# A gated recurrence feeding a SiLU MLP on one core: the planner that orders the instructions is replaced, and the DMA transposes begin at the eleventh unit

## The chip, the cores and the metric

The kernel runs on one NeuronCore of a Trainium2 chip. The metric is device microseconds of one execution, the median of several runs; lower is better. The core has four compute engines that run side by side, each strictly in the order in which its instructions stand: TensorE (PE, matrix multiplies), ScalarE (ACT, activations), VectorE (DVE) and GpSimd (POOL). SyncE (SP) computes nothing here; it issues DMAs. POOL issues DMAs too.

## The reference

Inputs `q`, `k`, `v`, `f_logit` are float32 of shape (4 batches, 8 heads, 768 steps, 48). The first part is a recurrence with a decay for each key row; its output becomes the input of an MLP with `w_in` (384 x 2048) and `w_out` (2048 x 384):

```python
f = 1.0 / (1.0 + np.exp(-f_logit))
for t in range(S):
    state = f[:, :, t, :, None] * state + np.einsum('bhd,bhe->bhde', k[:, :, t], v[:, :, t])
    y[:, :, t] = np.einsum('bhd,bhde->bhe', q[:, :, t], state)
x = y.transpose(0, 2, 1, 3).reshape(B * S, H * D)      # 3072 x 384
h = x @ w_in
out = (h * (1.0 / (1.0 + np.exp(-h)))) @ w_out          # 3072 x 384
```

## The kernel before, in words

**Units.** The 768 steps are cut into 6 chunks of 128, for each of the 4 batches: 24 units, numbered chunk by chunk, so that unit u needs the state that unit u-4 left. Two neighbouring units make a pair; there are 12 pairs. A unit is 128 rows of the MLP's input.

**What a unit does** (short names as in the planner, lines of the kernel before):
- four loads `f k q v` by SP (L390), 192 KB each;
- `E`, `L` on ACT: exp and log of `f_logit`, the log of the decay (L397, L399); for the first two pairs unit by unit, later for both units of a pair at once;
- `cs` on PE: running sums of that log by a triangular matrix, into the PSUM tile `cs`, of which there is one buffer (L445, L449);
- `ia`, `al`, `a` on ACT: the exponentials of those sums (L452, L456, L454); `a` writes back into the tile `cs`;
- `ki` and `vb` on POOL (k scaled, L458; v cast, L460); `qg` on DVE (q scaled, L462). `qg` is the last reader of the tile `cs`, so the next unit's `cs` waits for it;
- the scaled q and k turned by 90 degrees into `qkT`: either `tq` on PE (eight transposes, L468) and a copy `qkc` on DVE (L470), or `qkD`, one transposing DMA issued by SP (L472);
- `sc` on PE (scores, L479), `at` on DVE (mask, L483), `y` on PE (L488 for the part from the state, L492), `yc` on DVE (L496);
- y turned into `xT`: either `yT` on PE (L502) and `xc` on DVE (L504), or `xD`, a transposing DMA of SP (L498);
- `d` on PE (L510), `sd` on DVE (L515), `su` on POOL (L521): the state's update.

**The MLP.** For a pair (256 rows): eight tasks `mi` on PE, six matmuls of 256 columns each (L426), each followed by `si` on ACT, a SiLU of 128x512 (L422). Then for each unit four tasks `mo` on PE, four matmuls of 384 columns each (L436), a copy `oc` on DVE (L439) and a store `so` (L442), issued by POOL up to unit 17 and by SP from unit 18. The PSUM tile `mlp` has three buffers. `mi` tile j needs a quarter of `w_in`, `mo` step m a quarter of `w_out`: eight DMAs `wi`, `wo` of 384 KB issued by POOL (L409, L412).

**Tables.** Exp and log share one table of ACT, SiLU has another. Every change of kind on ACT puts a table load there (L549).

**Who sets the order.** A planner runs when the kernel is built. `make_tasks` (L61) lists all tasks with their engine, an assumed cost and their dependences; `schedule` (L174) plays a greedy list schedule: whenever an engine is free it takes the ready task of least priority number. A priority is a due time: `pace` (3.66 in the kernel before) times the unit's number plus an offset of the kind of task (`rank`). Buffers are given out in the same play. SP and POOL each have a ring of DMAs; where both have one under way, SP's gets 0.17 of the rate. `margin` is added on the way into PE. `planned` (L323) sorts the tasks by their planned start, and the kernel emits them in that order (L545), inside `tc.manual_schedule()`. What is handed to the chip is only the order on each engine, and which buffer each task uses: the chip waits on semaphores, not on planned times.

**Idle matmuls.** 70 matmuls on a tile of zeros (`warm`, L414) are tasks with the worst priority of all; PE takes one when it has nothing else, until they are used up. All stand before the first `mi`.

**Orders around the change, as built.** On SP the loads go `f0 k0 q0 v0 f1 k1 q1 v1 ...` up to `f12`, then turns (`qkD`, `xD`) stand between them. On POOL the weights stand after `vb2` (three of `wi`), after `su0` (`wi3`, `wo0`), after `su1` (`wo1`), after `ki4` (`wo2`) and after `vb6` (`wo3`): `w_after` in the configuration ties each to a `ki`. On ACT the `E` of a pair may stand ahead of an `a` or `L` that other work waits for: `ia17 E20 al17 a17`, `E16 E18 L16 L18 ia16`.

Of the kernel before, what the change touches and what calls it, by code (L numbers as in the profile page):

```python
# [21 lines left out]
NTILES = 16  # L22

CFG = dict(
    turned=8,
    turned_y=8,
    warm=70,
    warm_at=5.0,
    single=0,
    w_after=(2, 2, 2, 3, 3, 3, 4, 5),  # L30
    pace=3.66,
    margin=0.2,
    late_store=18,
    keep_exp=117.43,
    keep_silu=245.53,
    hold_exp=0.58,
    hold_silu=0.64,
    rank=dict(ld=-44.14, E=-215.27, cs=-365.49, ia=97.44, ki=-23.12, vb=175.4, qg=451.56, tq=-142.94, qkc=-77.52, sc=-74.11, at=-79.38, y=-7.63, yc=-223.81, yT=-176.78, xc=-369.47, d=13.22, sd=-254.14, su=26.79, mi=-117.59, si=-4.81, mo=20.95, mstep=0.47, oc=215.45, so=524.34, wi=23.7, wo=55.81),
# [5 lines left out]
ENGINES = ("PE", "ACT", "DVE", "POOL", "SP")  # L44
SEM = {"PE": 0.22, "ACT": 0.06, "DVE": 0.06, "POOL": 0.08, "SP": 0.0}
INTO_PE = 0.09
TABLE = 1.29


class Task:  # L50
    def __init__(self, name, eng, occ, lat, prio, deps=(), acq=(), use=(), mode=None, dma=0.0):
        self.name, self.eng, self.occ, self.lat, self.prio = name, eng, occ, lat, prio
        self.deps, self.acq, self.use, self.mode, self.dma = list(deps), list(acq), list(use), mode, dma
# [6 lines left out]

def make_tasks(cfg):  # L61
    T, tasks, pace, R = {}, [], cfg["pace"], cfg["rank"]
    extra = cfg.get("extra", {})

    def add(name, eng, occ, lat, prio, **kw):
        t = Task(name, eng, occ, lat, prio + extra.get(name, 0.0), **kw)
        T[name] = t
        tasks.append(t)
        return t
# [8 lines left out]
    base = lambda u: pace * u  # L78
    for n in range(cfg["warm"]):
        add(("warm", n), "PE", 0.107, 0.107, 1e6 + n, acq=[inst(("wm", n), "mlp")])  # L80
    for u in range(UNITS):
        P = u // 2
        for n, x in enumerate("fkqv"):
            add((x, u), "SP", 0.45, 0.45, base(u) + R["ld"] + n * 0.1, acq=[inst((x, P), x)], dma=0.875)

    for P in range(PAIRS):
        us_list = [(2 * P,), (2 * P + 1,)] if P < 2 else [(2 * P, 2 * P + 1)]
        for us in us_list:
            occ, lat = (0.43, 0.54) if len(us) == 1 else (0.74, 0.85)
            e = add(("E", us), "ACT", occ, lat, base(us[0]) + R["E"], deps=[T["f", u] for u in us], acq=[inst(("e", us), "e")],  # L90
                    use=[I["f", P]], mode="exp")
            add(("L", us), "ACT", occ, lat, base(us[0]) + R["E"] + 0.1, deps=[e], acq=[inst(("lf", P), "lf")],
                use=[I["e", us]], mode="exp")
    log_of = lambda u: T["L", (u,)] if u < 4 else T["L", (u - u % 2, u - u % 2 + 1)]

    for u in range(UNITS):
        c, b, P, B = u // BATCHES, u % BATCHES, u // 2, base(u)
# [5 lines left out]
        occ = 0.162 + (0 if last else 0.1)  # L103
        cs = add(("cs", u), "PE", occ, occ, B + R["cs"], deps=[log_of(u)], acq=[I["cs", u]], use=[I["lf", P]])
        ia = add(("ia", u), "ACT", 0.387, 0.49, B + R["ia"], deps=[cs], acq=[I["ia", u]], use=[I["cs", u]], mode="exp")
        if not last:
            al = add(("al", u), "ACT", 0.08, 0.173, B + R["ia"] + 0.1, deps=[cs], acq=[I["al", u]], use=[I["cs", u]], mode="exp")
        a = add(("a", u), "ACT", 0.387, 0.486, B + R["ia"] + 0.2, deps=[ia], use=[I["cs", u]], mode="exp")
        ki = add(("ki", u), "POOL", 0.94, 0.994, B + R["ki"], deps=[ia, T["k", u]], acq=[I["qk", u]], use=[I["ia", u], I["k", P]])
        vb = add(("vb", u), "POOL", 0.445, 0.503, B + R["vb"], deps=[T["v", u]], acq=[I["vb", u]], use=[I["v", P]])  # L110
        qg = add(("qg", u), "DVE", 0.47, 0.554, B + R["qg"], deps=[a, T["q", u]], acq=[I["qk", u]], use=[I["cs", u], I["q", P]])
        if u >= cfg["turned"]:
            qkT = add(("qkD", u), "SP", 0.6, 0.6, B + R["tq"], deps=[qg, ki], acq=[I["qkT", u]], use=[I["qk", u]], dma=1.3)
        else:
            tq = add(("tq", u), "PE", 0.444, 0.444, B + R["tq"], deps=[qg, ki], acq=[I["tq", u]], use=[I["qk", u]])
            qkT = add(("qkc", u), "DVE", 0.61, 0.692, B + R["qkc"], deps=[tq], acq=[I["qkT", u]], use=[I["tq", u]])
        sc = add(("sc", u), "PE", 0.425, 0.33, B + R["sc"], deps=[qkT], acq=[I["sc", u]], use=[I["qkT", u]])
        at = add(("at", u), "DVE", 1.2, 1.29, B + R["at"], deps=[sc], acq=[I["atm", u]], use=[I["sc", u]])
        yd = [at, vb] + ([T["su", u - BATCHES]] if c else [])
        y = add(("y", u), "PE", 0.38 if c else 0.21, 0.38 if c else 0.21, B + R["y"], deps=yd, acq=[I["y", u]],  # L120
                use=[I["atm", u], I["vb", u], I["qkT", u]] + ([I["st", u - BATCHES]] if c else []))
        yc = add(("yc", u), "DVE", 0.475, 0.558, B + R["yc"], deps=[y], acq=[I["yb", u]], use=[I["y", u]])
        if u >= cfg["turned_y"]:
            xc = add(("xD", u), "SP", 0.4, 0.4, B + R["yT"], deps=[yc], acq=[I["xT", P]], use=[I["yb", u]], dma=0.6)
        else:
            yT = add(("yT", u), "PE", 0.167, 0.167, B + R["yT"], deps=[yc], acq=[I["yT", u]], use=[I["yb", u]])
            xc = add(("xc", u), "DVE", 0.27, 0.358, B + R["xc"], deps=[yT], acq=[I["xT", P]], use=[I["yT", u]])
        T["x", u] = xc
        if not last:
            d = add(("d", u), "PE", 0.168, 0.168, B + R["d"], deps=[ki, vb, y], acq=[I["d", u]], use=[I["qk", u], I["vb", u]])  # L130
            sdd = [d] + ([T["su", u - BATCHES]] if c else [])
            sd = add(("sd", u), "DVE", 0.464, 0.551, B + R["sd"], deps=sdd, acq=[I["sd", u]],
                     use=[I["d", u]] + ([I["st", u - BATCHES]] if c else []))
            add(("su", u), "POOL", 1.01, 1.07, B + R["su"], deps=[sd, al], acq=[I["st", u]], use=[I["sd", u], I["al", u]])

    for n in range(4):
        add(("wi", n), "POOL", 0.8, 0.8, R["wi"] + n, deps=[T["ki", cfg["w_after"][n]]], dma=2.36)
    for n in range(4):
        add(("wo", n), "POOL", 0.8, 0.8, R["wo"] + n, deps=[T["ki", cfg["w_after"][4 + n]]], dma=2.5)

    for P in range(PAIRS):
        B = base(2 * P + 1)
        single = P < cfg["single"]
        for j in range(NTILES // 2):
            us = [(2 * P + i,) for i in range(2)] if single else [(2 * P, 2 * P + 1)]
            pass
        parts = [(2 * P,), (2 * P + 1,)] if single else [(2 * P, 2 * P + 1)]
        per = 4 if single else 2
        done = {}
        for us in parts:  # L150
            for j in range(NTILES // per):
                h = inst(("h", us, j), "mlp")
                deps = [T["x", u] for u in us] + [T["wi", (j * per) // 4]]
                off = 0.0 if len(us) == 2 else (us[0] - 2 * P - 1) * pace
                mi = add(("mi", us, j), "PE", 0.655, 0.655, B + off + R["mi"] + j * R["mstep"] * per / 2, deps=deps,
                         acq=[h], use=[I["xT", P]])
                done[us, j] = add(("si", us, j), "ACT", 0.476, 0.597, B + off + R["si"] + j * R["mstep"] * per / 2, deps=[mi],
                                  acq=[I["hT", P]], use=[h], mode="silu")
        for i in range(2):
# [3 lines left out]
            for m in range(4):  # L163
                need = [done[us, m]] if single else [done[us, 2 * m], done[us, 2 * m + 1]]
                mo = add(("mo", u, m), "PE", 0.648, 0.648, B + R["mo"] + (4 * i + m) * R["mstep"],
                         deps=need + [T["wo", m]] + ([T["mo", u, m - 1]] if m else []), acq=[o], use=[I["hT", P]])
            oc = add(("oc", u), "DVE", 0.468, 0.552, B + R["oc"] + 4 * i, deps=[mo], acq=[inst(("ob", u), "o")], use=[o])
            late = u >= cfg["late_store"]
            add(("so", u), "SP" if late else "POOL", 0.35 if late else 0.58, 0.5, B + R["so"] + 4 * i, deps=[oc], use=[I["ob", u]],
                dma=0.6)  # L170
# [3 lines left out]
def schedule(tasks, slots, cfg, fixed=None):  # L174

    margin = cfg["margin"]
    for i, t in enumerate(tasks):
        t.idx, t.start, t.end, t.succ, t.ready, t.left = i, None, None, [], 0.0, len(t.deps)
    for t in tasks:
        for d in t.deps:  # L180
            d.succ.append(t)
        for x in dict.fromkeys([*t.acq, *t.use]):
            x.users, x.slot = 0, None
    for t in tasks:
        for x in dict.fromkeys([*t.acq, *t.use]):
            x.users += 1
    free = {c: [(0.0, s) for s in range(n)] for c, n in slots.items()}
    busy = dict.fromkeys(ENGINES, 0.7)
    busy["PE"], busy["ACT"], busy["POOL"] = 1.3, 2.0, 1.9
    waiting = {e: [t for t in tasks if t.eng == e and not t.deps] for e in ENGINES}  # L190
    at = dict.fromkeys(ENGINES, 0)
    st = dict(mode="exp", last=2.0)
    ring = {"SP": [], "POOL": []}
# [386 lines left out]
```

## Time and profile before

| | |
|---|---|
| median of 3 runs | 204.59 us (204.46 to 205.04) |
| the profiled execution: its own time | 205.16 us |
| its span, first to last instruction | 203.3 us |
| mean granted PE clock | 0.938 of full |
| busy of the span: PE, ACT, DVE, POOL | 179.0, 121.3, 87.3, 72.5 us |
| SP's DMA queue (loads, turns, late stores): packets' time, share of 16 engines | 70.2% |
| POOL's DMA queue (weights, stores) | 14.8% |
| table loads on ACT inside the plan | 15, 19.2 us |

A busy share is the part of the span in which an engine had an instruction under way. PE's share holds the idle matmuls (10.1 us) and time at a reduced clock, so 179.0 us is not all useful work. An instruction's mean duration on PE holds its latency; what a row of matmuls costs one after another is read from the chain of work that ended last, which gives the time of each stretch (9.17 us for 84 matmuls of L426, for example). The profiled execution took 0.57 us more than the median.

### The profile page before, as it was taken

To read this page: it belongs to the slowest core of one execution; us is meant where nothing else is said; L and a number is where in the kernel's file an instruction comes from. 1 tells how busy PE (TensorE), PEld (TensorE's weight loads), DVE (VectorE), ACT (ScalarE), POOL (GpSimd) and SP (SyncE) were. 2 spreads that over 40 slices of the span, in tenths; PEclk is the share of its full clock that TensorE was granted. 3 is DMA by queue.
4 is the path that set the end of the run, shared out by engine and by line. 5 is a ranking of instruction groups with operands and counts; after the bars stand their busy time and mean duration, and the time that the engine had idled before them with its cause. 6 is when DMAs were issued, how large, how long until landed. Compare 5 with 4: busy or idle time off the path is not lost.

```text
span 203.3 us, 4480 instructions
## 1 busy us (share of the span) xinstructions
PE 179.0 (88%) x1766; PEld 131.1 (64%) x1766; DVE 87.3 (43%) x170; ACT 121.3 (60%) x208; POOL 72.5 (36%) x122
## 2 busy tenths in 40 slices
PE   7985889946999999969998997669979999999992
PEld 5764568734687678648567864438748678867850
DVE  4279261037264753872723064233845561162021
ACT  4646228962278769867739966186759767801700
POOL 2449603152181573383047004491167151000000
PEclk9997579995599999999999999969999999999998
DMA  6999999999999699999897999889899294003012
GB/s 133 204 193 173 191 189 195 204 200 187 204 221 236 120 166 247 197 185 191 175 221 156 161 194 187 188 187 213 160 234 156 80 115 112 0 16 118 25 42 77
DMA packets 129140, 32.80 MB, mean 161 GB/s; under 512 B 123904, under 2 KB 128256, under 8 KB 129120
## 3 DMA queue, kind: packets, MB, share of 16 engines
q1 hardware_dynamic: 124256, 25.83, 70.2%
q0 software_dynamic: 4864, 6.69, 14.8%
q8 instruction: 14, 0.23, 0.5%
q14 instruction: 6, 0.05, 0.1%
HBM read 25.17 MB, written 4.72 MB: 147 GB/s over the span
## 4 chain that ended last, share of the span: by engine, by line
PE 57%; DMA 13%; SPq 6%; ACT 3%; issue 2%; DVE 2%; POOL 0%; DVEq 0%; ACTq 0%
PE mlp L426 26%; PE mlp L436 23%; DMA f<-in_f_logit_dram 5%; SPq L390 5%; DMA xT<-yb 4%; DMA w_out_sb<-in_moe_w_out_dram 3%; PE sc L479 2%; PE yd L488 2%; ACT e L397 1%; PE yd L492 1%; PE cs L445 1%; SPq L498 1%; DVE qk L462 1%; DVE o L439 1%; PE yd L510 1%
## 5 line engine op out<-in xcount | busy, mean ns | idle before, releaser
L422 ACT ACTIVATE hT<-mlp 128x512 bf16<-128x512 f32 x96 | 56.6, 597 | 27.9 <-PE mlp L426 23.9
L436 PE MATMUL mlp<-w_out_sb,hT 128*128 128x384 bf16 x384 | 71.6, 333 | 1.8 <-DMA w_out_sb<-in_moe_w_out_dram 1.8
L426 PE MATMUL mlp<-xT,w_in_sb 128*128 128x256 bf16 x576 | 69.9, 280 | 2.7 <-DMA xT<-yb 1.3
L426 PEld LDWEIGHTS <-w_in_sb 128*128 128x128 bf16 x576 | 56.6, 100 | 12.6 <-DMA xT<-yb 2.0
L483 DVE TENSOR_TENSOR atm<-sc,triu 128x512 bf16<-128x512 f32 x48 | 30.9, 685 | 45.0 <-PE sc L479 44.8
L436 PEld LDWEIGHTS <-hT 128*128 128x128 bf16 x384 | 35.4, 99 | 22.8 <-issue 3.3
L458 POOL TENSOR_TENSOR qk<-k,ia 128x384 bf16<-128x384 f32 x24 | 23.9, 997 | 29.8 <-ACT al L456 22.2
L452 ACT ACTIVATE ia<-cs 128x384 f32<-128x384 f32 x24 | 11.7, 489 | 26.4 <-PE cs L449 20.5
L460 POOL CAST vb<-v 128x384 bf16<-128x384 f32 x24 | 12.0, 503 | 42.4 <-DMA v<-in_v_dram 29.5
L521 POOL TENSOR_TENSOR st<-sd,al 48x192 bf16<-48x192 f32 x40 | 20.1, 502 | 18.5 <-DVE sd L515 9.6
L462 DVE TENSOR_TENSOR qk<-q,cs 128x384 bf16<-128x384 f32 x24 | 13.2, 550 | 24.3 <-ACT cs L454 23.5
L439 DVE COPY o<-mlp 128x384 f32<-128x384 f32 x24 | 13.2, 554 | 18.6 <-PE mlp L436 18.5
L549 ACT ACT_TABLE_LOAD x15 | 19.2, 1283 | 0.3
L397 ACT ACTIVATE e<-f 128x768 f32<-128x768 f32 (+1 forms) x14 | 10.5, 750 | 14.6 <-DMA f<-in_f_logit_dram 14.6
L445 PE MATMUL cs<-lf,triu 128*128 128x384 bf16 x24 | 8.1, 339 | 9.9 <-DVE qk L462 6.6
L496 DVE CAST yb<-yd 128x384 bf16<-128x384 f32 x24 | 13.3, 552 | 6.7 <-PE yd L492 5.1
L449 PEld LDWEIGHTS <-lf 128*128 128x128 bf16 x80 | 5.0, 98 | 12.3 <-issue 10.7
L442 POOL DMA_DIRECT2D out_dram<-o x18 | 10.4, 580 | 5.3 <-DVE o L439 4.1
L454 ACT ACTIVATE cs<-cs 128x384 f32<-128x384 f32 x24 | 11.4, 477 | 0.6
L515 DVE TENSOR_TENSOR sd<-yd,st 128x384 f32<-128x384 f32 x16 | 8.8, 552 | 6.9 <-issue 2.9
L479 PE MATMUL sc<-qkT 48*128 48x128 bf16 x192 | 10.4, 233 | 1.1 <-DVE qkT L470 1.0
L414 PE MATMUL mlp<-idle 128*128 128x256 bf16 x70 | 10.1, 299 | 1.1 <-DVE idle L533 1.1
(35 smaller groups left out, 112.3 us busy)
## 6 DMA issues: line engine op xcount, KB each, us to landing
f<-in_f_logit_dram SPq DMA_DIRECT2D x24, 192.0 KB, 3.9
k<-in_k_dram SPq DMA_DIRECT2D x24, 192.0 KB, 4.1
q<-in_q_dram SPq DMA_DIRECT2D x24, 192.0 KB, 4.0
v<-in_v_dram SPq DMA_DIRECT2D x24, 192.0 KB, 4.0
out_dram<-o POOLq DMA_DIRECT2D x18, 192.0 KB, 3.7
w_in_sb<-in_moe_w_in_dram POOLq DMA_DIRECT2D x4, 384.0 KB, 9.1
w_out_sb<-in_moe_w_out_dram POOLq DMA_DIRECT2D x4, 384.0 KB, 9.5
out_dram<-o SPq DMA_DIRECT2D x6, 192.0 KB, 2.0
```

The source lines that it names most:

```text
L397: nc.scalar.activation(e, at("f", u // 2)[:, i:i + n], AF.Exp, scale=-1.0)
L422: return nc.scalar.activation(at("hT", P)[:, per * j:per * (j + 1), lo:hi], h, AF.Silu)
L426: nc.tensor.matmul(h[:, i, :], w_in_sb[:, kk, n * 128:(n + 1) * 128], at("xT", P)[:, kk, lo:hi], start=(kk == 0), stop=(kk == KT - 1))
L436: nc.tensor.matmul(o, at("hT", P)[:, n, i * C:(i + 1) * C], w_out_sb[:, n, :], start=(n == 0), stop=(n == NT - 1))
L439: nc.vector.tensor_copy(at("ob", u), at("o", u)[:, 0:d_model])
L458: nc.gpsimd.tensor_mul(at("qk", u)[:, 1, :, 0:D], at("k", P)[:, i], at("ia", u))
L462: nc.vector.tensor_mul(at("qk", u)[:, 0, :, 0:D], at("q", P)[:, i], at("cs", u)[:, 0:HD].rearrange("p (h d) -> p h d", d=D))
L479: nc.tensor.matmul(a_ps[:, r, p, :], qkT[lo:lo + D, 1, p, :], qkT[lo:lo + D, 0, p, :], start=True, stop=True)
L483: nc.vector.tensor_mul(at("atm", u)[:, r], at("sc", u)[:, r], triu[:, None, :].to_broadcast([C, NP, C]))
L496: nc.vector.tensor_copy(at("yb", u), at("y", u))
L521: nc.gpsimd.tensor_mul(at("st", u)[lo:lo + D, :, r * D:(r + 1) * D], at("sd", u)[lo:lo + D, :, r * D:(r + 1) * D], at("al", u)[lo:lo + D, ...
L549: nc.scalar.preload_act_table_set(tables[turn[id(t)]])
```

## The change

The planner is written anew, and so is its configuration. Emission is the same but for one name. What differs in the program that comes out:

- **Turns.** `turned=8`, `turned_y=8` become `range(10, 24)` twice: units 8 and 9 turn q, k and y on PE and DVE again, units 10 to 23 by DMA. 16 + 16 transposing DMAs become 14 + 14.
- **First two pairs unit by unit.** `single=0` becomes 2: pairs 0 and 1 take the MLP's first layer for one unit at a time. A `mi` is then twelve matmuls of 128 columns for four of the sixteen tiles of `w_in`, instead of six of 256 columns for two; the number of `si` (8 a pair, 128x512) stays. `mi` j of a unit needs the j-th quarter of `w_in`.
- **Weights.** `w_after` is gone. By the planned release times in `rel`, the order on POOL becomes `ki2 su0 wi1 wo0 wi3 ki3 vb2 su1 wi2 vb3 su2 wi0 wo1 su3 ki4 vb4 wo2 ki5 wo3`.
- **Loads.** `f`, `k`, `q`, `v` have ranks of their own. On SP: `f0 f1 q0 f2 k0 v0 q1 f3 k1 v1 q2 f4 k2 v2 q3 f5 k3 v3 q4 f6 k4 v4 ...`; the first turn stands after `k13`.
- **Idle matmuls.** They are no longer tasks: the play adds one when PE is idle and a modelled clock gate asks for it. 73 stand in the program, 72 of them in twelve groups before the first `mi`, one after it.
- **ACT.** 20 table loads in all instead of 16, the one at the start included: SiLU's runs are interrupted more often, once for `ia5` alone (`si2(1) ia5 si3(1)`).
- **The model** inside the play: each DMA has a service time, a time until it may start and a landing time; SP's issues cost more; PE's tasks take twice as long while a modelled clock is below 0.6. None of it is on the chip; it only changes the order.

```diff
 CFG = dict(
-    turned=8,
-    turned_y=8,
-    warm=70,
-    warm_at=5.0,
-    single=0,
-    w_after=(2, 2, 2, 3, 3, 3, 4, 5),
-    pace=3.66,
-    margin=0.2,
...
+    single_logs=2,
+    single=2,
     late_store=18,
+    turned=range(10, 24),
+    turned_y=range(10, 24),
...
+    rel={"wi_0": 24.53, "wi_1": 16.7, "wi_2": 21.23, "wi_3": 18.44, "wo_0": 17.53, "wo_1": 25.87, "wo_2": 38.86, "wo_3":
+         40.89},
+    pace=35.61,
...
+    margin=0.08,
 )
...
+LOAD = dict(ring=0, svc=0.95, elig=1.2, land=0.75)
+QKD = dict(ring=0, svc=1.25, elig=1.25, land=1.1)
+YD = dict(ring=0, svc=0.6, elig=1.2, land=0.75)
...
-            add((x, u), "SP", 0.45, 0.45, base(u) + R["ld"] + n * 0.1, acq=[inst((x, P), x)], dma=0.875)
+            add((x, u), "SP", 0.62, 0.62, "ld" + x, u, off=n * 0.1, acq=[inst((x, u // 2), x)], dma=LOAD)
...
-            qkT = add(("qkD", u), "SP", 0.6, 0.6, B + R["tq"], deps=[qg, ki], acq=[I["qkT", u]], use=[I["qk", u]], dma=1.3)
+            qkT = add(("qkD", u), "SP", 1.25, 1.25, "qkD", u, deps=[qg, ki], acq=[I["qkT", u]], use=[I["qk", u]], dma=QKD)
...
-        add(("wi", n), "POOL", 0.8, 0.8, R["wi"] + n, deps=[T["ki", cfg["w_after"][n]]], dma=2.36)
+        add(("wi", n), "POOL", 0.8, 0.8, "wi", off=n, dma=W_IN)
...
+        key = short(t.name)
+        t.ready = rel.get(key, 0.0)
+        t.prio = cfg["pace"] * t.um + cfg["rank"][t.rank] + t.off + cfg["mstep"] * t.mm + extra.get(key, 0.0)
...
+    def wants_warm():
+        if WARM_FROM <= now < WARM_ALL:
+            return True
+        past = now - win
+        return now < WARM_TO and clock > 0.6 and past > 0.8 and load_of(win, now) < WARM_SHARE * past
...
+        while win + WINDOW <= now + 1e-9:
+            share = load_of(win, win + WINDOW) / WINDOW
+            clock = 1.0 if share >= UP else 0.5 if share <= DOWN else clock
+            win += WINDOW
...
-            return nc.tensor.matmul(at("wm", rest[0])[:, 0:256], idle[:, 0:128], idle, start=True, stop=True)
+            return nc.tensor.matmul(at("warm", rest[0])[:, 0:256], idle[:, 0:128], idle, start=True, stop=True)
```

The tiles, their shapes, the buffer counts (`SLOTS`) and every other line of the emission are the same. Lines after the change lie 39 higher (L390 is L429, L426 is L465, L436 is L475, L472 is L511).

## The prediction, made before the changed kernel was run

> **What bounds the kernel now.** I read the busy rows of the page first, then stretches of the span, then PE's waits, then the chain that ended last.
>
> ```profile
> span 203.3 us, 4480 instructions
> ...
> PE   7985889946999999969998997669979999999992
> ...
> PEclk9997579995599999999999999969999999999998
> ```
>
> PE has work nearly throughout, but not at its rate: digits below 9, and clock digits of 5, are lost time. To size it I add up PE's useful work from rows of the chain in which matmuls run back to back.
>
> ```profile
> 167.76 9.17 PE mlp L426 x84
> ...
> 191.58 7.81 PE mlp L436 x48
> ```
>
> That is 0.109 us a matmul of L426 and 0.163 of L436. In the same way a unit's `sc` costs 0.33, `y` 0.48 (0.20 in the first chunk), `d` 0.17, `cs` 0.24 (0.16 in the last chunk), `tq` 0.45, `yT` 0.17. Sum: 576 x 0.109 + 384 x 0.163 + 24 x 0.33 + 10.4 (`y`) + 20 x 0.17 + 5.4 (`cs`) + 8 x 0.62 = 157.5 us. So 203.3 - 157.5 = 45.8 us of the span are lost on PE. Where (work by these prices, against the clock): before the first `mi` at 22.05, 17.2; from there to `cs4` at 41.6, 3.7; to `tq7` at 57.9, 8.4; to the last matmul at 199.4, 12.6; after it, 3.9 (copy, store, landing).
>
> ```profile
> 17.00:22.00 5.00, 2.56 (x31) 1.82 (x28) 3.98 (x8) 2.31 (x4) 4.77 (x8) 0.55 1.08 169
> ...
> 41.60:50.20 8.60, 4.13 (x54) 3.13 (x53) 5.49 (x9) 3.65 (x8) 3.94 (x5) 0.68 1.12 193
> 50.20:58.00 7.80, 7.76 (x61) 4.84 (x61) 3.14 (x8) 3.24 (x7) 2.68 (x4) 0.69 1.13 207
> ...
> 130.00:139.00 9.00, 5.42 (x43) 3.41 (x41) 2.16 (x4) 5.64 (x10) 5.57 (x9) 0.81 0.99 202
> ...
> 152.00:199.40 47.40, 47.38 (x435) 34.68 (x434) 15.81 (x28) 25.25 (x41) 8.65 (x14) 1.00 0.38 77
> ```
>
> Columns: stretch, its length, busy us of PE, PE's weight loads, DVE, ACT, POOL, then granted clock, DMA share, GB/s. From 152 on PE is full at full clock: nothing to gain there. Before, PE idles 4.5 us of 8.6, then runs 7.8 us busy with the clock partly at half; the DMA engines are full (about 1.0 and more) up to 150. What ends those waits:
>
> ```profile
> PE cs L445 <- DVE qk L462: 6.6, 3, 3.6
> PE cs L445 <- ACT lf L399: 3.4, 6, 1.5
> ```
> ```profile
> 42.50 0.94 POOL qk L458
> 43.43 6.76 DMA w_out_sb<-in_moe_w_out_dram
> 50.19 0.04 issue
> 50.24 1.44 PE mlp L436 x4
> ...
> 128.53 3.48 DMA f<-in_f_logit_dram
> 132.01 0.02 issue
> 132.04 0.84 ACT e L397
> ```
>
> Two causes. A quarter of `w_out` stands on POOL behind `ki4`, is issued at 43.43 and lands at 50.19, when `mo` wants it. And `E` of a later pair stands on ACT ahead of an `a` that `qg`, and so the single `cs` buffer, waits for: when the load of `f` is late, ACT stops, then PE at `cs`. It happens three times: `f` lands at 122.90, 132.01 and 148.81 by the chain.
>
> **The change, part by part.**
>
> *Start, to the end of the four units' first layer.* `f1 q0 f2` now go ahead of `k0`, and `su0` ahead of the first `wi`. `k2` is the 13th load, not the 10th; ACT's wait for the 13th ended at 15.46. `ki2` 1.0, `su0` 1.1: first `wi` issued at 17.6, not 15.21. The first one took 6.8 us to arrive (`mi` began at 22.05), so 24.4. By the trace's landing events pieces followed each other by 2.5 us: `wo0` 26.9, `wi3` 29.4, `wi2` 31.9, `wi0` 34.4, `wo1` 36.9. The last quarter's `mi` of four units (2.6), `tq4` and `sc4` end at 37.8; I take 39, for matmuls at half clock as in 22-28 now (ends 37.8 and 41). Work done by then: 18.0 us, which the kernel before reaches at 37.53 + (18.0 - 16.7) = 38.8. **Gain 0** (-2 to +1).
>
> *Weights `wo2`, `wo3`.* Wanted at 39 + 5.7 and 39 + 9.3 by the PE work ahead of them. `wo2` stands on POOL behind `vb4`, whose load is the 22nd, and `ki5` and `wo3` stand behind it. While weights moved, loads crawled: SP's issues then took 3.44, 5.91, 4.62 and 3.61 us, against 0.7 else. If `v4` lands at 32, `wo2` is there at 39.4; `ki5` lets `wo3` go at about 41.8, there at 48.6: a stall of 0 to 1. Attention of units 4 to 7 stands farther ahead now (16 us of PE work from `cs5` to `sc5`, 1.9 before). Of 8.4 lost I keep 2 (0 to 8.4). **Gain 6.4.**
>
> *Loads of `f` and the place of `E`.* I lay SP's list end to end at 0.95 us a load (0.7 to 1.2 between landings), 1.25 and 0.6 a turn, 2.4 a weight, 0.5 a store, and compare with PE's useful work up to the ACT task. Before, `E18`, `E20`, `E22` stood 8, 9 and 11 us ahead of the earliest arrival of `f19`, `f21`, `f23`; after, 0 and 1 ahead, and 5 behind. `f19` is SP's 79th DMA instead of the 91st. So the three waits should shrink: idle before `cs` at 120-125 (1.5), 130-135 (3.6, and 1.5 of half clock after it) and near 151 (1.2), 7.8 in all. Waits for turned y remain (1.7 at 85-92, 1.5 at 100-109). From `y` to the pair's first `mi` a turn needs 0.48 + 0.2 + 0.56 + 1.2 + 3.4 (its landing) = 5.8 us of other PE work; after, the list leaves 5.9, 6.3, 5.8, 6.4, 5.2, 6.0: about as tight. `sc21` has 6.7 us behind `cs21`, where some 6.6 are needed. I count 0.5 more there. **Gain 7.3** (0 to 10).
>
> *Units 8 and 9 on PE.* Two `tq` (0.45) and two `yT` (0.17): +1.24 on PE, all on the path, as PE is the bound there. DVE +2 x (0.69 + 0.35), beside 45 us of idle before its mask. SP is spared 2 x (1.28 + 1.2) of issuing, the DMA engines 3.7: counted in the item before. If PE is not the bound there, 0. **-1.2.**
>
> The row first: two `tq` ran at 57.9 and 60.3 and the granted clock was 1.00 from 55 to 65. The Trainium skill, "TensorE: Matmul & The Clock Gate", Part 4, says PE-mode transposes do not count as PE-busy in the same way, and Part 1 gives a window of about 3.4 us; by that rule each of the units 8 and 9 could cost a window at half rate, by my estimate from its figure 1.7 us each, and the sum would be 195.8. The row speaks for no such loss, as the transposes stand among matmuls.
>
> *`mi` by single units.* 192 matmuls of 128 columns for 96 of 256; eight of 128 columns (L468) take 0.45, so 12 take 0.68 against 0.655: 16 x 0.02 = **-0.3** (0 to -1). *Tables.* Four more at 1.28 = 5.1 us of ACT, 60% busy and idle 27.9 us before the SiLUs for want of PE. The two around `ia5` (2 x 1.28 + 0.49) fall between `wi1` and `wi3`, 5 us apart; without that cover +3. *Idle matmuls*: 73 for 70, where PE waits; 0 (0 to +0.4).
>
> Sum: 0 + 6.4 + 7.3 - 1.2 - 0.3 = 12.2. The profiled execution took 205.16, so 193.0 for one like it; it lay 0.57 above the median, so **192.4** beside 204.59.
>
> A second way to it: if `f21` arrives at 116.9 (DMA end to end) plus holes in the queue, 63.4 us of PE work and 3.9 follow `E20`: 184.2 + holes. Holes were 9.1 by `f21` before (132.0 against 122.9). None to 9.1 gives spans of 184 to 193, times of 185.5 to 194.6 (median less span is 1.3).
>
> **Rivals.**
> - *The weights are late again.* If `v4` and `k5` crawl as loads did beside the weights now (landings at 24.2, 30.3, 35.2), `wo2` goes out at 37 and takes the median 9.5, `wo3` lands past 50; PE stops at `mo`, the clock halves, and most of the 8.4 stays: about 198. For: the queue still puts loads behind weights. Against: the first weight moves 2.4 us later, when some 20 loads are through, not 16.
> - *Every link holds.* First layer done at 38, no stall: 186 to 189. Against: many links have under 1 us of spare, by my sums.
> - *Slower: turns hold SP, and `f` starves.* SP is in order: a turn that waits for `qg` or `ki` holds all loads behind it. Before, the waits for turns of q, k added to 16 us and those for y to 11. If the 14 later turns hold it 16 us longer, `f23` lands at 148.8 + 16 - 3.7 = 161; behind it stand 1.7 of ACT, 40.1 of PE and 3.9: 206.8, as time 208. It decides once `f23` lands after 157.6. For: turns now stand where the queue has run ahead less. Against: the list puts a turn 4 to 10 us behind its `qg` by PE's work.
> - *Nothing moves*: the DMA queue, full up to 150, sets the pace, and only its order changes: 204 to 205. Against: even at today's arrival of `f23` less 3.7, 145.1 + 45.7 = 190.8 is possible.
>
> **How the numbers follow.** About 0.3% is what a measurement here can tell from no change. Forecast (189 to 196) 0.60; late weights or other stalls (196 to 203.9) 0.18; every link holds 0.10; within 0.3% 0.03; slower 0.09. So faster 0.88. The range 186.5 to 200.5 leaves out the slower cases, no change, and the edges of the two others, under 0.2.
>
> **What would show it.** Right: `E` of late pairs waits under 1 us for `f`; `cs` waits far less than 10 us in all; no stop at `mo` for `w_out` over 1 us; clock 1.0 from 40 on; first `mi` near 24. Wrong: `f23` landing after 150, `mo` waiting for `w_out` near 45-50, clock digits of 5 past 45, long SP waits at L511.

## The result, and the profile after

| | before | changed |
|---|---|---|
| median of 4 runs, same chip | 204.81 us (204.46 to 205.94) | 194.56 us (193.00 to 195.47) |
| ratio, 95% interval | | 0.948 (0.940 to 0.957) |
| the profiled execution: time, span | 205.16, 203.3 us | 193.68, 191.5 us |
| mean granted PE clock in it | 0.938 | 1.000 |

The changed kernel is 5.2% faster. The forecast was 192.4 us, with a range of 186.5 to 200.5. A ratio here compares the undisturbed runs, so it need not be the quotient of two medians of all runs.

First the page of the changed kernel: its head, PE's busy digits and its clock digits.

```profile
span 191.5 us, 4715 instructions
...
PE   7886777999999999999999994998999799999991
...
PEclk9999999999999999999999999999999999999999
```

From the eighth slice (some 34 us) on PE's digits are 9 but for three slices and the last, and the clock is never reduced. Before, digits of 4 to 8 came as late as the 30th slice. Next the same stretches as for the kernel before (columns as there: stretch, length, busy us of PE, PE's loads, DVE, ACT, POOL, then clock, DMA share, GB/s).

```profile
17.00:22.00 5.00, 3.61 (x58) 2.72 (x55) 4.04 (x9) 2.89 (x6) 4.85 (x8) 1.00 1.02 182
...
41.60:50.20 8.60, 8.49 (x98) 5.78 (x96) 5.81 (x12) 5.56 (x12) 2.53 (x6) 1.00 1.14 203
50.20:58.00 7.80, 7.80 (x90) 6.58 (x89) 4.13 (x8) 5.34 (x9) 5.32 (x9) 1.00 1.08 251
...
130.00:139.00 9.00, 8.40 (x81) 6.92 (x80) 2.14 (x5) 6.56 (x12) 1.09 (x2) 1.00 0.87 178
```

In 41.6 to 50.2 PE now executes 98 matmuls where it executed 54, in 50.2 to 58.0 it executes 90 instead of 61, and in 130 to 139 it is busy 8.40 us of 9 instead of 5.42. The DMA share in the first two stays where it was (1.12 and 1.13 before): the transfers are as dense, but PE no longer stops for them. PE's waits, in us in total, times, and the longest:

```profile
PE sc L518 <- DMA qkT<-qk: 4.2, 3, 2.6
PE cs L484 <- DVE qk L501: 1.8, 3, 0.8
PE mlp L465 <- DMA w_in_sb<-in_moe_w_in_dram: 1.2, 1, 1.2
...
PE cs L484 <- ACT lf L438: 0.2, 1, 0.2
```

The waits at `cs` fell from 6.6 + 3.4 to 1.8 + 0.2 (what is left of them after 21 us is one of 0.23), and a wait of `mo` for `w_out` is not listed at all. At the head of the list stands a new one: `sc` waits for a turn of q and k by DMA. The chain that ended last, in order of time, shows where (start, length, what):

```profile
112.78 6.57 DMA qkT<-qk
...
141.81 4.91 DMA v<-in_v_dram
...
148.60 3.64 DMA qkT<-qk
```

The turn for unit 17 took 6.57 us from its issue to its landing, and PE stood 2.59 us before `sc17`. The second place, near 149, is one turn behind the last load: `v23` lands at 146.73, and `sc20` and `sc21` wait 1.19 and 0.46 us.

**Where the 11.8 us of the span came from.** I use the prediction's prices for a matmul, and call the span less PE's useful work *lost*. Useful work is 157.5 before and 158.7 after (units 8 and 9). The prediction names the transpose at 57.9 `tq7`; by the order on PE it is `tq6`, and `tq7` follows at 60.2, with PE at its rate in between, so the point serves as it stands.

| stretch | lost before | lost after | gain | forecast |
|---|---|---|---|---|
| start, to 18.0 us of PE work | 20.8 (at 38.83) | 22.1 (at 40.09) | -1.3 | 0, less 0.3 for single `mi` |
| from there to `tq6` before (57.9), `tq7` after (57.6) | 8.4 | 0.35 | +8.0 | +6.4 |
| from there to the last matmul (199.4; 187.6 after) | 12.6 | 6.5 | +6.1 | +7.3 |
| more PE work | | | -1.2 | -1.2 |
| after the last matmul | 3.9 | 3.9 | 0 | 0 |
| sum | | | 11.6 | 12.2 |

The 0.2 between 11.6 and the 11.8 of the spans is rounding of prices.

The same span can be cut at the landing of the last load, `v23`: before at 151.50, with 51.8 us behind it; after at 146.73, with 44.7 behind it. Cut there, 4.8 us lie in the DMA queue ending sooner, and 7.1 in PE having less left to do when it did.

### The profile page after: what moved, and what is told of

The parts are those of the page before. It is cut to its first block, busy times and chain, and to the rows that moved or that the text cites. A ratio compares the mean times of both kernels' runs of the same rounds, so it can differ in the third digit from the quotient of the medians.

```text
span 191.5 us, 4715 instructions
## 1 busy us (share of the span) xinstructions
PE 173.7 (91%) x1887; PEld 130.3 (68%) x1887; DVE 90.3 (47%) x174; ACT 125.0 (65%) x212; POOL 72.6 (38%) x122
## 4 chain that ended last, share of the span: by engine, by line
PE 31%; DMA 10%; SPq 5%; ACT 2%; issue 1%; DVE 1%; POOL 1%; ACTq 0%; DVEq 0%; POOLq 0%
PE mlp L475 14%; PE mlp L465 12%; DMA qkT<-qk 5%; SPq L429 5%; DMA v<-in_v_dram 3%; DMA xT<-yb 3%; PE sc L518 1%; PE yd L531 1%; PE yd L527 1%; PE cs L484 1%; DVE o L478 1%; ACT hT L461 1%; POOL st L560 1%; ACT ia L491 1%; PE yd L549 0%
## 5 line engine op out<-in xcount | busy, mean ns | idle before, releaser
L465 PE MATMUL mlp<-xT,w_in_sb 128*128 128x256 bf16 (+1 forms) x672 | 69.1, 257 | 3.8 <-DMA w_in_sb<-in_moe_w_in_dram 1.2
L475 PE MATMUL mlp<-w_out_sb,hT 128*128 128x384 bf16 x384 | 70.9, 326 | 0.0
L465 PEld LDWEIGHTS <-w_in_sb 128*128 128x128 bf16 x672 | 56.6, 98 | 12.6 <-issue 1.8
L475 PEld LDWEIGHTS <-hT 128*128 128x128 bf16 x384 | 34.6, 97 | 18.9
L588 ACT ACT_TABLE_LOAD x19 | 24.4, 1283 | 0.3
L436 ACT ACTIVATE e<-f 128x768 f32<-128x768 f32 (+1 forms) x14 | 10.5, 748 | 9.5 <-DMA f<-in_f_logit_dram 9.5
L481 POOL DMA_DIRECT2D out_dram<-o x18 | 10.4, 577 | 11.9 <-DVE o L478 11.8
L518 PE MATMUL sc<-qkT 48*128 48x128 bf16 x192 | 9.5, 219 | 5.5 <-DMA qkT<-qk 4.2
L453 PE MATMUL mlp<-idle 128*128 128x256 bf16 x73 | 12.0, 309 | 1.1 <-DVE idle L572 1.1
L518 PEld LDWEIGHTS <-qkT 48*128 48x128 bf16 x192 | 5.4, 94 | 10.3 <-DMA qkT<-qk 5.8
L509 DVE COPY qkT<-tq 128x1024 bf16<-128x1024 bf16 x10 | 6.9, 686 | 11.7 <-PE tq L507 11.7
```

The source lines that it names most:

```text
L465: nc.tensor.matmul(h[:, i, :], w_in_sb[:, kk, n * 128:(n + 1) * 128], at("xT", P)[:, kk, lo:hi], start=(kk == 0), stop=(kk == KT - 1))
L475: nc.tensor.matmul(o, at("hT", P)[:, n, i * C:(i + 1) * C], w_out_sb[:, n, :], start=(n == 0), stop=(n == NT - 1))
L518: nc.tensor.matmul(a_ps[:, r, p, :], qkT[lo:lo + D, 1, p, :], qkT[lo:lo + D, 0, p, :], start=True, stop=True)
L588: nc.scalar.preload_act_table_set(tables[turn[id(t)]])
```

## The experiments

Theory: PE's stops at 41 to 58 (`w_out`) and at `cs` in 100 to 152 (`f` and the place of `E`) were two losses of their own, and the new order removes both. Rival: the queue of DMAs is full, so a transfer that is put ahead makes another late, and the gain belongs to the whole order and not to one of its moves.

Ten kernels came from one of the two orders by moving, adding or leaving out tasks in the finished list, or by planning again; one is the changed kernel again, one a sum of three edits. `put(order, a, b)` takes task a out of the list and puts it behind b. Each result stands beside runs of the kernel before on the same chip. Their median was 202.25 us (19 runs) for weights, place of `E`, idle matmuls and the three together; 202.81 (13 runs) for the loads of `f`, the new order without idle matmuls, and the turns from the 9th and 13th unit; 203.94 (17 runs) for the other four.

### The weights alone, in the old order

```diff
+    put(order, ("wo", 2), ("wo", 1))
+    put(order, ("wo", 3), ("wo", 2))
```

> The kernel before, with one edit: the third and fourth quarter of w_out are issued on POOL right behind the second, not behind ki4 and vb6. Theory of the prediction (the late weights cost most of the 8.4 us lost between 41.6 and 57.9): mo no longer waits for w_out, PE does not idle long enough there for the clock to fall, 5 to 7 us faster, about 198 to 200. Rival (the DMA queue is what is short): the two quarters now move between 35 and 40 and push back the loads of units 5 to 7 by some 5 us, so E4, cs4 and cs5 come late instead; 0 to 2 us faster, and PE's wait moves to cs.

Measured: 202.33 us (200.36 to 204.69, 10 runs), ratio 1.003 (0.998 to 1.008): no change. `wo2` and `wo3` landed at 38.10 and 40.76, and no wait for `w_out` is left. But `f5`, behind them, landed at 41.46 instead of 36.55. PE's waits of this kernel, and its stretch from 38 to 58:

```profile
PE cs L454 <- DVE qk L471: 5.9, 3, 2.8
PE cs L454 <- ACT lf L408: 4.0, 4, 2.4
```
```profile
38.00:58.00 20.00, 14.87 (x126) 9.60 (x124) 7.79 (x15) 8.93 (x18) 5.41 (x7) 0.74 1.04 203
```

The waits at `cs` did not fall (9.9 us for 10.0 before), and PE is busy 14.87 of 20 us at a clock of 0.74 (15.49 at 0.74 before). The weights came some 12 us earlier, and PE stopped for `f` instead, 2.35 us before `cs4` at 43.31. The theory of a loss on its own falls here, the rival's full queue stands.

### The place of `E` alone, in the old order

```diff
+    put(order, ("E", (18, 19)), ("a", 17))
+    put(order, ("E", (20, 21)), ("a", 19))
+    put(order, ("E", (22, 23)), ("a", 21))
...
+    put(order, ("cs", 22), ("y", 20))
```

Each `L` follows its `E`. The last line puts `cs22` behind `ia22`, so unit 22 is computed from sums that are not yet its own; that part of the computation is changed, the amount of work is not.

> The kernel before, with E and L of pairs 9, 10 and 11 put later on ACT (behind a17, a19 and a21), and cs22 put behind y20 on PE. The loads and their order are unchanged. Theory of the prediction (ACT stops at an E whose f has not landed, and holds an a that the single cs buffer waits for): idle before cs at 120-125, 130-135 and 151 shrinks from 6.3 us to 1 or 2 and the half clock after 130 goes, 4 to 6 us faster, about 199 to 200.5. Rival (the DMA queue sets the pace; f, k, q and the turns come late in any case): the waits move to sc and to qkT, under 1.5 us faster.

Measured: 204.36 us (202.71 to 205.79, 4 runs), ratio 1.015 (0.999 to 1.031): no gain. PE's waits of this kernel, in its longest run (205.79):

```profile
PE mlp L440 <- DMA xT<-yb: 4.3, 2, 3.2
...
PE cs L459 <- DVE qk L476: 1.8, 1, 1.8
```

The wait that the edit aims at is gone (1.8 for 6.6), and `mi` waits 4.3 us for a turned y instead (1.3 before).

### The loads of `f` alone, in the old order

```diff
+    for u in range(6, UNITS):
...
+        order.insert(next(i for i, x in enumerate(order) if x.name == ("k", u - 2)), t)
```

> The kernel before, with one edit: on SP every load of f from unit 6 on stands two units farther ahead (directly before k of the unit two earlier), as it does in the changed kernel; the order on all other engines is the same, the turns keep their places. The two runs before showed that moving weights alone only moves the wait from w_out to f (f5 landed at 41.5 in place of 36.6). Theory now: the DMA queue is full, and what counts is that f, the input with the longest chain behind it, is served first; then E never waits for f after 60, the waits at cs from 119 on go, f19 lands 5 us or more earlier, and the time falls by 3 to 6 us beside the kernel before. Rival: k, q and v come later by what f gains, ki and qg wait, and the turns with them: within 1.5 us of before.

Measured: 205.34 us (202.17 to 207.07, 10 runs), ratio 1.004 (0.998 to 1.010): no change. `f19` landed at 112.40 instead of 122.90, `f23` at 132.0 instead of 148.81. PE's waits:

```profile
PE mlp L437 <- DMA xT<-yb: 5.4, 2, 3.5
...
PE cs L456 <- DVE qk L473: 1.8, 1, 1.8
```

As with the place of `E`: `cs` waits far less (2.7 us in all, 10.0 before), and the turned y is late in its stead. Two different ways of taking away the late `f` end at the same next wait.

### More idle matmuls in the old order

33 more among the matmuls of units 0 to 3:

```diff
+    for n, (after, count) in enumerate([(("yT", 0), 3), (("sc", 1), 6), (("tq", 2), 4), (("y", 1), 4), (("sc", 2), 4),
+                                        (("yT", 1), 6), (("tq", 3), 6)]):
...
```

> The kernel before, with 33 more idle matmuls set between the attention steps of the first four units, where PE waits from 14 to 22 us; nothing else. The prediction counted idle matmuls at nothing: same time within 0.4 us. Rival (the granted clock of 0.5 from 18 to 28 delays the start of the MLP): the clock stays at 1.0 there, the first layer of the first two pairs ends earlier, 1 to 3 us faster.

Measured: 201.15 us (199.99 to 202.98, 10 runs), ratio 1.001 (0.996 to 1.007): no change. The stretches that had a clock of 0.55 (17 to 22) and 0.52 (22 to 28) before, in this kernel:

```profile
17.00:22.00 5.00, 4.26 (x58) 3.47 (x56) 3.73 (x7) 2.31 (x4) 4.77 (x8) 1.00 1.11 174
22.00:28.00 6.00, 4.08 (x55) 3.19 (x54) 3.13 (x6) 2.39 (x4) 1.85 (x4) 1.00 1.21 191
```

The full clock came, and no gain in time with it that the runs show. Where it was given back I can't read from the profile with certainty: that is of the shortest run (199.99), in which `cs` still waits 4.8 us for `qg` and `mo` 1.2 for `w_out`.

### The three edits together

Weights, place of `E` (with the same change of the computation) and idle matmuls in one kernel.

> The kernel before with the three edits together (weights behind one another, E later, 33 more idle matmuls). If they are independent and the prediction's causes are the right ones, the gains add up to most of the way to the changed kernel: 193 to 196. If the DMA queue takes the gains back, 198 to 203.

Measured: 205.88 us (202.62 to 206.85, 4 runs). No ratio is given, as the runs lie too far apart; even the shortest shows no gain. In the profiled run (205.92) `mi` waits 5.4 us for turned y and `cs` 5.3 for ACT. Three removals do not add up to a part of 11 us.

### Fewer turns, in the old order

```diff
-    turned=8,
-    turned_y=8,
+    turned=10,
+    turned_y=10,
```

> The kernel before with turned and turned_y 10 in place of 8, planned anew by the old planner with its own ranks. If the turns alone carried the change (3.7 us less in a full DMA queue), 2 to 4 us faster than the kernel before; if the order carries it, within 2 us of it.

Measured: 203.49 us (201.70 to 206.12, 10 runs), ratio 1.002 (0.997 to 1.006): no change. The old planner ran again, so the whole order differs. Its profile has `v23` landing at 141.72, 9.8 us earlier than before, and still a span of 200.8: 59.1 us of it come after the last load. `cs` waits 5.7 us for `qg`, `mo` 2.5 for `w_out`. So in this order an early end of the queue is worth little: the loads were there, and PE had not done its work meanwhile.

### The new order without most idle matmuls

Of the 73, the 29 from the 45th on are left out; these stand after `cs2`.

```diff
+    order = [t for t in order if t.name[0] != "warm" or t.name[1] < 44]
```

> The changed kernel without its idle matmuls from the 45th on (29 taken out, all those after cs2, which stand in PE's waits between 13 and 28 us). The prediction counted them at nothing: within 0.5 us of the changed kernel. Rival: they keep the granted clock at 1.0 through the start; without them it falls to 0.5 from about 18 to 30 as before the change, and the time rises by 2 to 4 us.

Measured: 198.51 us (195.73 to 198.79, 4 runs), ratio to the kernel before 0.975 (0.964 to 0.987), where the changed kernel has 0.948 (0.940 to 0.957): about half of the gain is gone, and all four runs lie above all eight of the changed kernel (190.74 to 195.47 in two sets). Its clock digits, and two of its stretches:

```profile
PEclk9995555899999999999999999999999999999999
```
```profile
17.00:22.00 5.00, 2.64 (x31) 2.02 (x32) 3.80 (x8) 2.78 (x6) 4.46 (x8) 0.50 1.09 186
...
28.00:38.00 10.00, 5.56 (x68) 4.81 (x68) 3.86 (x8) 3.87 (x5) 5.22 (x9) 0.61 1.11 191
```

The clock is 0.50 from 17 to 28 and 0.61 to 38, as the rival said. The loss in this profile comes by another way. `wi1` and `wi2` went out no later than in the changed kernel (17.08 and 22.43, there 17.66 and 22.62); `wi0` went out at 32.15 for 26.63. It stands on POOL behind `su2`. That task waits for `sd` of unit 2 on DVE, which stands there behind `qg4`, and `qg4` waits for the load `q4`:

```profile
31.13 1.07 POOL L568 TENSOR_TENSOR st<-sd,al 48x192 bf16<-48x192 f32 x2 [7.34 <-DVE sd L564]
```
```profile
30.02 0.56 DVE L509 TENSOR_TENSOR qk<-q,cs 128x384 bf16<-128x384 f32 x1 [6.17 <-DMA q<-in_q_dram]
```

So what came last there was not PE but `q4`, which landed at 29.93 and not at 24.41. SP issued it at 17.56, 0.48 us behind the first weight; in the six other profiles of the new planner's orders that issue stood 0 to 0.22 us ahead of the first weight, and `q4` landed 5.1 to 7.5 us later, not 12.4. With `wi0` behind it, `wo1` landed at 41.72 instead of 37.27 and `v23` at 151.26 instead of 146.73, both 4.5 us later, as the span is (196.1 for 191.5).

Two stretches of the control below, the changed kernel with all its idle matmuls, speak against the clock as the cause:

```profile
17.00:22.00 5.00, 3.35 (x37) 2.56 (x38) 3.90 (x8) 1.69 (x2) 4.85 (x8) 0.69 1.00 186
22.00:28.00 6.00, 5.96 (x84) 4.96 (x83) 3.90 (x9) 3.51 (x6) 4.33 (x9) 0.69 1.22 181
```

Its clock was reduced there too, `q4` landed 6.3 us after its issue, and its span is 190.4. A clock of 0.69 for 11 us thus cost nothing that shows. The deeper and longer reduction (0.50, then 0.61, up to 38) no run has by itself. Why the first weight overtook `q4`, and whether the missing idle matmuls bring that about in every execution, one profile does not tell.

### The new planner with turns from the 9th or the 13th unit on

```diff
-    turned=range(10, 24),
-    turned_y=range(10, 24),
+    turned=range(8, 24),
+    turned_y=range(8, 24),
```

and the same with `range(12, 24)`; both planned again, with all other numbers as in the changed kernel.

> The changed kernel with turned and turned_y from unit 8, planned anew by the same planner with the same ranks: two more turns of q, k and two of y in the queue, 1.24 us less on PE. Theory (DMA queue full to 146): 3.7 us more of service ahead of the last loads, and two chains longer by a turn's landing, 2 to 5 us slower than the changed kernel. The prediction's own price for this part was the other way: 1.2 us faster, as PE has less to do.

> The changed kernel with turned and turned_y from unit 12, planned anew with the same ranks: two turns of q, k and two of y less in the queue, 1.24 us more on PE. Theory (DMA queue full to 146): 3.7 us less service, 0 to 2.5 us faster than the changed kernel. By PE as the bound: 1.2 us slower. The ranks were not fitted to it, which can cost a us or two either way.

Measured: from the 9th unit 202.47 us (197.29 to 203.26, 4 runs), from the 13th 193.78 us (193.05 to 195.81, 4 runs), ratio 0.961 (0.952 to 0.970). No ratio is given for the first, as its runs lie too far apart: three at 202.4 to 203.3, one at 197.29. Even that one lies above every run of the changed kernel (190.74 to 195.47 in two sets). In its longest run, with a span of 201.2, `sc` waits 3.7 us for turns of q and k and `mi` 3.4 for turns of y, and `v23` lands at 156.24. From the 13th unit on `v23` lands at 142.12, 4.6 us earlier than in the changed kernel, and the span is the same 191.5: what the queue gives back does not reach the end; that the two units more on PE cost it is likely and not shown. Between a start of the turns at 10 and at 12 no difference is shown. At 8 the time is longer, but every kernel here has an order of its own, fitted to 10 only.

### The changed kernel again

> The changed kernel itself once more, as the measure for the two next on the same chip: 193 to 195.5.

Measured: 193.31 us (190.74 to 194.99, 4 runs), ratio 0.944 (0.934 to 0.955); profiled span 190.4, with clock digits of 5 and 7 in two slices of the start and 6 in one near 110. `cs` waits 3.8 us here, and `sc` for a turn is not among the first five waits. What the first profile shows at `sc17` is thus not fixed: single waits of 1 to 3 us differ between these two executions.

### The new order with the last loads behind two turns

```diff
+    for x, after in (("q", "qkD"), ("k", "q"), ("v", "k")):
+        put(order, (x, 23), (after, 21 if after == "qkD" else 23))
+    put(order, ("vb", 23), ("ki", 23))
```

> The changed kernel with four tasks moved: on SP the loads q23, k23, v23 stand behind the turn of unit 21 and not ahead of the turns of y18 and of units 20 and 21; on POOL vb23 stands behind ki23. In the changed kernel's trace y18 could be turned at 141.1 but its DMA was issued up to 145.8, behind those loads, and PE then waited 1.2 us at sc20 and 0.5 at sc21, with some 1.2 more before them. Theory (what counts is which transfer is next in the full queue): these waits go, v23 lands near 151 without harm, 1.5 to 2.5 us faster than the changed kernel. Rival (the loads that now come last are the bound): same time.

Measured: 195.04 us (192.02 to 195.85, 6 runs), ratio 0.950 (0.940 to 0.960), not to be told from the control. `sc20` and `sc21` ran without a wait, at 148.74 and 151.14; then `sc22` waited 0.98 at 155.24, and `mi` waited 3.0 for `w_in` (1.2 in the changed kernel). The 1.7 us aimed at did not come out at the end.

### The new order with `f` one unit later

```diff
+    for u in range(12, UNITS):
...
+        order.insert(next(i for i, x in enumerate(order) if x.name == ("k", u - 1) or x.name[0] == "E" and u in x.name[1]), t)
```

> The changed kernel with each load of f from unit 12 on put one unit later on SP, at the latest right ahead of the E that reads it; all else the same. The prediction's step (f must be there when E comes): E waits for f again from 90 us on, two or three waits at cs of 1 us and more, 2 to 4 us slower than the changed kernel. Rival, after the run with f moved ahead in the kernel before, which gained nothing: what f loses k and the turns gain, within 1 us of the changed kernel.

Measured: 206.48 us (206.03 to 208.29, 4 runs), ratio 1.019 (1.009 to 1.028): 13 us longer than the control and longer than the kernel before. This is the one edit that takes the whole gain away. PE's first wait and ACT's wait for `f` in this kernel, and its stretch from 100 to 120:

```profile
PE cs L495 <- DVE qk L512: 13.2, 5, 4.3
```
```profile
ACT e L447 <- DMA f<-in_f_logit_dram: 20.6, 6, 5.6
```
```profile
100.00:120.00 20.00, 14.35 (x138) 9.91 (x138) 7.92 (x15) 11.24 (x19) 6.05 (x10) 0.84 0.65 130
```

PE is busy 14.35 us of 20 (17.18 in the changed kernel), and now the DMA engines idle too: share 0.65 for 1.02. SP's own list shows why (start, length, instruction; here the transposes are turns):

```profile
96.71 5.55 SPq L522 DMA_TRANSPOSE qkT<-qk  x2
...
105.45 0.86 SPq L440 DMA_DIRECT2D k<-in_k_dram  x1
110.42 1.18 SPq L548 DMA_TRANSPOSE xT<-yb  x1
...
112.80 0.58 SPq L440 DMA_DIRECT2D f<-in_f_logit_dram  x1
```

`f17` lands at 97.63, and until then ACT stands 5.63 us. So `a`, `qg` and the second of the two turns are late, and the turn holds SP until 102.3. PE waits for the same `qg` too, 4.04 us before `cs15` at 101.02, and y of unit 12, which stands behind that on PE, comes late: its turn holds SP again from 106.3 to 110.4, and `f19`, behind that turn, goes out at 112.80 only. A late `f` makes the next `f` late: the lag grows around the loop of load, ACT, PE, turn and SP. In the changed kernel `f17`, `f19`, `f21` and `f23` land at 90.94, 104.95, 122.43 and 138.36; here at 97.63, 117.08, 136.74 and 153.24, so the lag goes from 6.7 to 14.9 us.

## Why the prediction was right, and where its terms were off

The direction and the kind of the gain were right, and the time of the profiled run was met within 0.7 us (193.0 forecast for one like it, 193.68 measured). The median is 2.2 us above the forecast. Of this 0.6 is in the sum of terms; the rest comes from taking 0.57 off, because the profile of before lay above its median. The profile of the changed kernel lay 0.9 below its own.

- **Start, 0 forecast (-0.3 with the single `mi`, which stand there), -1.3 measured.** The arrivals were right nearly to the tenth: first `wi` issued at 17.66, landed at 24.39 (17.6 and 24.4 forecast), the others at 27.20, 29.66, 32.11, 34.62 and 37.27. The step that failed is "the last quarter's `mi` of four units (2.6), `tq4` and `sc4`" behind `wi0`. When `wi0` landed at 34.62, PE still had matmuls of the quarter before: 101 matmuls of 128 columns ran between 33.32 and 40.09, of which 48 are the last quarter's, with PE busy 6.03 us of the 6.1 from 34 on and at full clock. The 39 allowed for a half clock; the clock was full and the queue of work was longer. Most of the difference is a term that the prediction had put at nothing, the two table loads around `ia5`: it counted them as covered between `wi1` and `wi3`, but they and `ia5` held ACT from 28.52 to 31.61, and `wi3` had landed at 29.66. SiLU, and with it the PSUM tiles that PE needs, came late, and PE stood 1.01 us before 32.26 (1.01 in the control too):

```profile
32.26 4.85 PE L465 MATMUL mlp<-xT,w_in_sb 128*128 128x128 bf16 x84 [1.01 <-ACT hT L461]
```

- **Weights, +6.4 forecast, +8.0 measured.** The mechanism held, one of its inputs did not: `v4` landed at 37.84 and not at 32, later even than the last of the three landings (35.2) that the rival of late weights went by. `wo2` and `wo3` went out at 38.34 and 41.60 and landed at 44.23 and 47.68, in 5.9 and 6.1 us, where the rival took 9.5 and the kernel before had 6.8 for the one that PE waited for. That is 0.5 and 0.6 before the 44.7 and 48.3 at which I had PE wanting them, and PE came there a little later. PE was not stopped, and the 2 of 8.4 that I kept as lost did not occur.
- **`f` and the place of `E`, +7.3 forecast, +6.1 measured.** `cs` waits 2.0 us for 10.0. I said `E` of late pairs would wait under 1 us for `f`. ACT's groups of `E` in the changed kernel (start, length, [wait and its end]):

```profile
105.03 0.84 ACT L436 ACTIVATE e<-f 128x768 f32<-128x768 f32 x1 [0.62 <-DMA f<-in_f_logit_dram]
122.46 0.84 ACT L436 ACTIVATE e<-f 128x768 f32<-128x768 f32 x1 [3.01 <-DMA f<-in_f_logit_dram]
141.01 0.83 ACT L436 ACTIVATE e<-f 128x768 f32<-128x768 f32 x1
```

  That was wrong of `E20`, with 3.01. It cost PE nothing: it was busy 5.00 us of the 5 from 120 to 125, as the wait no longer stands before an `a` that `cs` needs. The missing 1.2 lies in the turns. `sc` waits 4.2 us for them in all, of which I counted 0.5 ("`sc21` has 6.7 us"): the turn of unit 17 took 6.57 us to land. The waits for turned y gave 2.4 of these 3.7 back: I kept 3.2 (1.7 and 1.5), and 0.8 were left. What was tight was not where I looked.
- **Units 8 and 9, -1.2.** Priced right as PE work. The granted clock was 1.00 from 65 to 70, where `tq8` and `tq9` ran, in the profiled run and in the control, so no loss of clock came with them. The rule of the Trainium skill, "TensorE: Matmul & The Clock Gate", Part 4, from which the prediction worked out its estimate of 195.8 us, found no support here. That the queue gains in return was seen only for the next two units: with turns from unit 12 on PE has 1.24 us more to do, `v23` lands 4.6 us earlier, and the span is the same.
- **Idle matmuls, 0 (0 to +0.4): the term with the least behind it.** "Where PE waits; 0" prices three more of them and not their places, which are new. Without 29 of them the kernel takes some 4 us more. The profile of that run puts the loss on the load `q4` behind the first weight, not on PE's clock, and the control has a reduced clock at the start without a loss.
- **The second way.** 184.2 plus the holes in the queue: `f21` landed at 122.43 instead of 116.9, so 5.5 of holes, 189.7 for a span of 191.5. It bounded the result better than its range of 0 to 9.1 let me hope.
- **The rivals.** Late weights did not occur, the slower case neither: SP's two longest sums of waits at turns of q, k are 4.7 and 3.0 us, 9.3 and 4.8 before. But its mechanism is real, and the experiment that puts `f` one unit back shows it, at 206.5 us against the 208 I gave it: `f23` landed at 153.24, not after 157.6, and it had cost the gain already. "Nothing moves" fell with `v23` at 146.73. In the old order, though, no single edit moved the time; that the reason is a full queue, in which one transfer gives way to another, the landings show for the weights (`f5` at 41.46 for 36.55).

**What the sum hid.** I added terms as if each were a loss that one edit takes away. In the old order none of them was: weights, place of `E`, lead of `f`, idle matmuls and fewer turns gave ratios of 1.003, 1.015, 1.004, 1.001 and 1.002 one by one. The waits of the profile are right, but behind each stood the next one: `f` behind the weights, the turned y behind `f` and `E`. So that the sum came within 0.6 of what was measured is in part luck: weights 1.6 better than their term stand against a start 1.0 and `f` 1.2 worse, and all were priced as if they did not touch each other. Which set of moves is the least that carries the gain, I have not found: the runs show that each of these five alone does not, that three of them together do not, that without the lead of `f` the new order has no gain, and without 29 idle matmuls half of it. The new order of the first loads and weights, and the single `mi`, no run takes apart.

What stays open: how the 29 idle matmuls bear on `q4` and the first weight; whether turns from the 13th unit on are better or worse by some 1%; and how much of the ratio is owed to the execution, as repeated runs of one kernel on one chip spread by 0.7 to 3.0%.

## What to carry to other kernels

A wait in a profile tells what was last and not what would be gained: before taking it as a term, look for the transfer that stands behind it in the same full queue, and count only the distance to the next wait. Where an in-order queue holds loads behind transfers that need computed data, a late load returns as a later load: here a lag of 6.7 us at `f17` was 14.9 at `f23`. And when an edit costs time, follow the chain of waits back before naming the part that was edited as the cause: without the idle matmuls the clock fell, as expected, but the wait that carried the loss was for a load that had gone out half a us behind a weight.

## What the runs showed of the hardware

- The landing of a 192 KB load depends on what stands around it. `v4`, behind weights, was issued at 20.33 and landed at 37.84, 17.5 us later; `v23` took 4.9 us. SP took 5.77 us to issue `v4` and 0.97 to issue `v23`. `q4` took 5.1 to 7.5 us where its issue stood 0 to 0.22 us ahead of the first weight (six profiles), and 12.4 where it stood 0.48 behind (one profile).
- A turn of q and k took 3.6 us to land at 148.60 and 6.57 us at 112.78, in a stretch (100 to 120) with a DMA share of 1.02.
- From 17 to 22 us the granted clock was 1.00 in one profile of the changed kernel and 0.69 in another, with PE busy 3.61 and 3.35 us of 5 and the same idle matmuls; without 29 of them it was 0.50 at 2.64 of 5, and with turns from the 13th unit 0.50 at 4.13 of 5.
- Eight executions of the changed kernel had mean clocks of 0.971 to 1.000 and spans of 188.4 to 193.2 us; the span does not go by the clock alone (190.4 at 0.971, 192.5 at 0.997).
- The kernel before had medians of 202.25, 202.81, 203.94 and 204.81 us in four sets of runs, 1.3% apart, so that only runs beside each other are compared here.
